# A two-layer attention and Mish network on one core: the opening of the first block rewritten, x fetched first, the queries' weights folded by raw chunks as they land

## The chip, the cores and the metric

The kernel runs on one core of one Trainium2 chip. The time is the device time of one execution in microseconds (us), as a median over several runs. The profile is of one execution of its own; its times count from the start of its span. The engines are named as the profile names them: PE is TensorE (PEld its weight loads), DVE VectorE, ACT ScalarE, POOL GpSimd, SP SyncE, which issues the DMAs.

## What is computed

Two equal layers, each an attention part and a dense part, on x of 2048 rows by 640 columns, all in float32:

```python
# attention, 32 heads of 20
q, k, v = split(layernorm(x) @ wqkv)
pq, pk  = q @ w_phi[h], k @ w_phi[h]             # per head, 20 x 20
phi     = concat(softmax(p), softmax(-p))        # 40 features a head, for pq and pk
kv, z   = phi_k.T @ v, phi_k.sum(rows)
o       = (phi_q @ kv) / (phi_q @ z + 1e-6)
x       = x + o @ wo
# dense
h = layernorm(x) @ w1 + b1                       # 1536 wide
x = x + (h * tanh(softplus(h))) @ w2
```

## The kernel before

**Tiles and parts.** The rows are worked on in 8 blocks of 256, each of two tiles of 128 rows. Every large product is done in three: each operand is split into a high part (a rounded copy by ACT) and a low part (what is left, subtracted on DVE, or on POOL for some weights), and PE adds high x high, high x low and low x high (`project_half`, L338, the matmuls at L344). One half of a projected tile is 320 columns and 5 x 3 = 15 matmuls. The rows are normed (`norm_stats` on DVE, `norm_scale` on POOL and DVE, then an ACT instruction a tile), turned on PE against the identity (`Transposed.step`, L271, transposes at L280: three steps of 4, 4 and 2), and split at L285 (`xth`, ACT) and L286 (`xtl`, DVE).

**Folding.** w_phi acts per head on q and k, so it is multiplied into their weights beforehand. `load_raw` (L212) fetches the transposed raw weights of q or k in 6 chunks: five of 120 rows (6 heads) and one of 40 rows (2 heads). `bd` holds w_phi as block-diagonal matrices, one per chunk, in six column groups of 120. `fold_phi` (L227) multiplies, for each of five k (128 rows of the weights) and for each of two halves c (three chunks each: 360 and 280 columns), a chunk by its matrix into PSUM (L237; a float32 product shows as two instructions), and then makes the high part (L242, ACT) and the low part (L243, DVE). It is run twice in layer 0: for q in the opening, and for k inside block 0. The v weights aren't folded: `load_v_weights` (L167) fetches five pieces and `split` (L123) makes the parts on ACT (L127) and DVE (L128).

**Passes.** `attend_first` (L387) goes through the blocks and makes, per tile, keys (`k`), queries (`q`) and values (`v`), in the order that `order` gives: a projection of 30 matmuls each, and for keys and queries the feature steps of `features` (L355: maxima and subtractions, an exp, sums and a scaling on DVE, POOL and ACT; the queries' first subtraction, L369, and all scalings, L379, are on POOL). The queries' features go to memory. `advance` moves the features of earlier tiles on by one step each time. Within a block, its third step norms the next block, and the later steps turn it. At the end of block 1 the folded weights are spilled and the five pieces of the output weights `wo` are fetched and split (`make_five`, L193, `make_parts`: ACT at L148, POOL at L149). `attend_second` reads the queries' features back (`average`, L569), and `dense` (L677) does the rest; neither is touched.

**Order.** The whole is planned by a scheduler that orders each engine's instructions by a simulated timeline at compile time. Where the program says `manual_schedule(engines=...)`, the named engines keep the order in which the lines stand; instructions from outside such a part can still come between. In the opening of before that holds for SP alone, so that only the DMAs are in the written order. `act` (L110) chains most of the ACT instructions one behind the other. Buffers: 5 `big`, 4 row tiles (`xn`), 2 `v`, 2 `x`; in PSUM 2 double banks `mm` and 4 single ones `one`.

The opening of before (L446 to L460), in the order of its DMAs: half of `bd`, raw chunks 0 to 2 of q, x of block 0, the rest of `bd`, chunks 3 to 5, the v weights, the raw chunks of k. The norm of block 0 comes between, then its three turning steps, the folding of q, and the parts of v, as the scheduler orders them.

Of the kernel before, what the change touches and what calls it, by code (L numbers as in the profile page):

```python
# [1 line left out]

# [6 lines left out]
F32 = mybir.dt.float32  # L9
# [32 lines left out]
def kernel(  # L42
# [25 lines left out]
    def one_tile():  # L68
        return psum.tile([P, 512], F32, tag="one", name="one", bufs=4)
# [35 lines left out]
    x1_d = dram.tile([S, D], F32, name="x1_d")  # L105
    x2_d = dram.tile([S, D], F32, name="x2_d")

    last_act = [None]

    def act(*args, **kw):  # L110

        if last_act[0] is None:
            ins = nc.scalar.activation(*args, **kw)
        else:
            with tc.issue_after(last_act[0]):
                ins = nc.scalar.activation(*args, **kw)
# [6 lines left out]
    def split(hi, lo, src, stage):  # L123

        st = stage()[:, :D]
        nc.sync.dma_start(st, src)
        nc.scalar.activation(hi, st, AF.Copy)  # L127
        nc.vector.tensor_tensor(lo, st, hi.bitcast(F32), op=ALU.subtract)  # L128

# [31 lines left out]
    def r2_pair(j):  # L161
# [2 lines left out]
            return w[:, 0], w[:, 1]  # L164
        return tuple(wts.tile([P, D], F32R, tag=f"r2{s}{j}", name=f"r2{s}{j}") for s in "hl")

    def load_v_weights():  # L167

        ws = [r1_pair(k) for k in range(KD)]
        for k in range(KD):  # L170
            split(ws[k][0][:, D:2 * D], ws[k][1][:, D:2 * D], wv[k * P:(k + 1) * P, :],
                  (row_tile, row_tile, v_tile, v_tile, big_tile)[k])
        return ws

    def load_q_weights():
# [36 lines left out]
    def load_raw(which, ts=range(6)):  # L212

        raw = []
        for t in ts:
            rows = 120 if t < 5 else 40
            if t < 5:
                r = wts.tile([P, D], F32, tag=f"r2{'hl'[which]}{5 + t}", name=f"raw{which}{t}")
            else:
                r = r2_wide(10 + which, F32)[:, 0]  # L220

            n = P if t < 5 else rows
            nc.sync.dma_start(r[:n], wqk_t[which * D + t * 120:which * D + t * 120 + n, :])
            raw.append((r, rows))
        return raw

    def fold_phi(ws, bd, raw):  # L227

        pss = {}
        for k, c in ((0, 0), (1, 0), (2, 0), (3, 0), (0, 1), (1, 1), (2, 1), (3, 1), (4, 0), (4, 1)):  # L230
            if c == 0:
                mm = None if k % 2 else mm_tile()
                pss[k] = [one_tile(), one_tile()] if k % 2 else [mm[:, 0], mm[:, 1]]
            ps = pss[k][c]
            for t in range(3 * c, 3 * c + 3):
                r, rows = raw[t]
                nc.tensor.matmul(ps[:, (t % 3) * 120:(t % 3) * 120 + rows],  # L237
                                 r[:rows, k * P:(k + 1) * P], bd[:rows, t, :rows],
                                 start=True, stop=True)
            n0, n1 = (0, 360) if c == 0 else (360, D)  # L240
            hi, lo = ws[k][0][:, n0:n1], ws[k][1][:, n0:n1]
            nc.scalar.activation(hi, ps[:, :n1 - n0], AF.Copy)  # L242
            nc.vector.tensor_tensor(lo, ps[:, :n1 - n0], hi.bitcast(F32), op=ALU.subtract)  # L243


    def norm_stats(t, xt):
# [135 lines left out]
    def fetch(x_src, b, xt=None):  # L382
        xt = x_tile() if xt is None else xt
        nc.sync.dma_start(xt, row_block(x_src, b))
        return xt

    def attend_first(layer, x_src, first):  # L387


        def fetch_normed(b):  # L390
            if layer:
                return load_turned(n2_d[b], [row_tile] * 3)
            xt = fetch(x_src, b)
            norm_scale(b, [norm_stats(t, xt) for t in range(BT)])
            return xt

# [9 lines left out]
        def keys(xts, i, v):  # L406
            e = big_tile()
            yield from features(project(xts, i % BT, kv_ws, 0), e, False)
            yield
            if i % BT == 0 and BT < i < NT - BT:  # L410
                yield
            for r in range(9):
                for j in range(4):
                    h = 3 * (4 * (r // 3) + j) + r % 3
                    if h < H:
                        nc.tensor.matmul(kva[32 * j:32 * j + DH + 1, 40 * r:40 * r + 40],  # L416
                                         v[:, (DH + 1) * h:(DH + 1) * (h + 1)], e[:, 40 * h:40 * h + 40],
                                         start=(i == 0 and r == 0), stop=(i == NT - 1), skip_group_check=True)
# [25 lines left out]
            yield  # L444

        if first is None:  # L446
            with tc.manual_schedule(engines={mybir.EngineType.SP}):
                bd = big_tile()[:120, :720].rearrange("p (t c) -> p t c", t=6)
                nc.sync.dma_start(bd[:, :3], phi_bd[:, :3])
                raw = load_raw(0, range(3))  # L450
                xt = fetch_normed(0)
                nc.sync.dma_start(bd[:, 3:], phi_bd[:, 3:])
                raw += load_raw(0, range(3, 6))
                nxt = normed(0, xt).all()
                q_ws = [r2_pair(k) for k in range(KD)]
                fold_phi(q_ws, bd, raw)
                kv_ws = load_v_weights()
                raw = load_raw(1)
            nc.sync.dma_start(mask, bass.AP(tensor=head_mask.tensor, offset=head_mask.offset,
                                            ap=[[1, 120], [120 * (DH + 1), 3]]))  # L460
        else:
            nxt, kv_ws = first
            load_k_weights(kv_ws)
            q_ws = load_q_weights()
        for b in range(NB):
            xts = nxt
            order = ("k0", "k1", "v0", "v1", "q0", "q1")
            if b == 0 and layer:
                order = ("v0", "k0", "k1", "v1", "q0", "q1")
            elif b == 0:  # L470
                order = ("v0", "q0", "v1", "k0", "q1", "k1")
            elif b == 1 and not layer:
                order = ("k0", "q0", "k1", "v0", "q1", "v1")
            elif b == NB - 1:
                order = ("k0", "k1", "v0", "v1", "q0")
            vs = [v_tile() for _ in range(BT)]
            for n, (kind, t) in enumerate(order):
                t = int(t)
                i = b * BT + t
                if b == 0 and n == (1 if layer else 3):  # L480
                    if layer == 0:
                        fold_phi(kv_ws, bd, raw)
                    kva = one_tile()
                    nc.vector.memset(kva[:, :360], 0.0)
                if b == NB - 1 and n == 3:
                    loaded = {0: load(0)}
                if b + 1 < NB:
                    if n == 0:
                        xt = fetch_normed(b + 1)
                    elif n == 2:  # L490
                        nxt = xt if layer else normed(b + 1, xt)
                    elif n > 2:
                        nxt.step()
                g = {"k": lambda: keys(xts, i, vs[t]), "q": lambda: queries(xts, i),
                     "v": lambda: values(xts, i, vs[t])}[kind]()
# [399 lines left out]
```

## Time and profile before

| | us |
|---|---|
| median of 3 runs (1381.08 to 1383.7) | 1382.19 |
| the profiled execution's own time | 1381.04 |
| its span | 1379.0 |
| busy in it: PE, DVE, ACT, POOL | 1364.3, 1077.0, 583.3, 441.0 |
| first instruction of PE starts at | 4.42 |
| PE's first long projection work (L344) starts at | 18.61 |

A busy time is the sum of an engine's instructions; those of PE are pipelined, with modelled ends, so a busy PE isn't PE at its peak, and instructions of one kind are better compared from start to start. Rows of instructions in order of time give start, duration, engine, line, operation, output and input names, shapes, count, and in brackets the idle time before them with what ended it. Rows by stretches give, per engine, busy time and count, and then the granted PE clock, the DMA engines' share and GB/s. A DMA row has the time that SP takes to issue it; "to landing" counts from that issue to the arrival.

### The profile page before, as it was taken

What the parts mean: (1) busy time and instruction counts of PE and PEld (TensorE: products, weight loads), DVE (VectorE), ACT (ScalarE), POOL (GpSimd) and SP (SyncE); (2) the same over time, 40 slices, a digit from 0 to 9 for tenths busy, and PEclk for the clock granted to TensorE, in tenths of its full rate; (3) what the DMA queues carried; (4) which work ended last, traced back from release to release, by engine and by line L of the source; (5) the groups of instructions that cost most, each with busy time, mean ns of one, the idle gap of its engine ahead of it and who ended that gap; (6) DMA issues with size and microseconds to landing.
All of it is one profiled execution on the core that took longest, in us unless ns stands there. A gap on an engine that the chain in (4) does not pass through costs nothing.

```text
span 1379.0 us, 30804 instructions
## 1 busy us (share of the span) xinstructions
PE 1364.3 (99%) x12866; PEld 1350.7 (98%) x12866; DVE 1077.0 (78%) x1820; ACT 583.3 (42%) x971; POOL 441.0 (32%) x334
## 2 busy tenths in 40 slices
PE   7999999999999999999999999999999999999998
PEld 7999999999999999999999999999999999999998
DVE  5799977886698887788769898988668776677775
ACT  4444434222355444545454333432235444354443
POOL 1353543353322221222234434453342111111112
PEclk9999999999999999999999999999999999999999
DMA  8532433779624533344473433458965321333200
GB/s 321 173 67 62 73 54 61 211 227 316 227 68 96 115 90 62 80 116 96 117 262 74 95 59 59 70 117 274 297 239 163 77 53 45 97 96 96 77 20 19
DMA packets 350277, 169.67 MB, mean 123 GB/s; under 512 B 287098, under 2 KB 323690, under 8 KB 350138
## 3 DMA queue, kind: packets, MB, share of 16 engines
q1 hardware_dynamic: 350137, 167.72, 45.0%
q8 instruction: 100, 1.64, 0.5%
q14 instruction: 40, 0.32, 0.1%
HBM read 104.76 MB, written 62.91 MB: 122 GB/s over the span
## 4 chain that ended last, share of the span: by engine, by line
PE 94%; DVE 2%; DMA 1%; issue 1%; POOL 0%; SPq 0%; ACT 0%; DVEq 0%; POOLq 0%; ACTq 0%
PE mm L344 26%; PE one L691 24%; PE mm L733 24%; PE one L344 12%; PE mm L569 3%; PE one L280 2%; PE one L416 2%; PE mm L237 1%; DMA raw<-in_wqk_t 1%; DVE m L368 1%; PE one L237 0%; DMA v<-in_wv 0%; DVE big L371 0%; DVE r L377 0%; DMA raw<-in_wo 0%
## 5 line engine op out<-in xcount | busy, mean ns | idle before, releaser
L733 PE MATMUL mm<-r2h,ol 128*128 128x320 f32 x1280 | 305.0, 309 | 0.3 <-ACT ol L716 0.3
L717 POOL TENSOR_TENSOR ol<-big,ol 128x512 fp32r<-128x512 f32 (+1 forms) x98 | 130.4, 1330 | 483.6 <-ACT ol L716 407.4
L691 PE MATMUL one<-xtl,r1h 128*128 128x256 f32 x960 | 268.2, 279 | 0.0
L691 PE MATMUL one<-xth,r1l 128*128 128x256 f32 x960 | 268.0, 279 | 0.0
L691 PE MATMUL one<-xth,r1h 128*128 128x256 f32 x960 | 265.9, 279 | 0.0
L733 PEld LDWEIGHTS mm<-r2h,ol 128*128 128x128 f32 x1280 | 219.2, 188 | 0.6 <-ACT ol L716 0.6
L733 PE MATMUL mm<-r2l,ol 128*128 128x320 f32 x640 | 197.3, 309 | 0.0
L344 PE MATMUL mm<-r1h,xth 128*128 128x320 f32 x600 | 187.5, 312 | 0.0
L344 PE MATMUL mm<-r1h,xtl 128*128 128x320 f32 x600 | 185.8, 310 | 0.4 <-DVE xtl L286 0.4
L344 PE MATMUL mm<-r1l,xth 128*128 128x320 f32 x600 | 186.0, 310 | 0.0
L691 PEld LDWEIGHTS one<-xtl,r1h 128*128 128x128 f32 x960 | 180.4, 188 | 0.0
L691 PEld LDWEIGHTS one<-xth,r1l 128*128 128x128 f32 x960 | 180.4, 188 | 0.0
L691 PEld LDWEIGHTS one<-xth,r1h 128*128 128x128 f32 x960 | 179.6, 188 | 0.0
L706 DVE TENSOR_SCALAR big<-big 128x512 f32<-128x512 f32 (+1 forms) x98 | 56.4, 575 | 110.6 <-ACT big L704 110.4
L379 POOL TENSOR_TENSOR r<-r,r 128x1280 f32<-128x1280 f32 x32 | 76.6, 2395 | 154.3 <-DVE r L378 148.5
L733 PEld LDWEIGHTS mm<-r2l,ol 128*128 128x128 f32 x640 | 120.2, 188 | 0.0
L708 ACT ACTIVATE big<-big,two 128x512 f32<-128x512 f32 (+1 forms) x98 | 70.3, 717 | 116.0 <-DVE big L707 116.0
L704 ACT ACTIVATE big<-one,b1s 128x256 f32<-128x256 f32 x192 | 81.0, 468 | 90.1 <-PE one L691 89.6
L716 ACT ACTIVATE ol<-big 128x512 fp32r<-128x512 f32 (+1 forms) x98 | 61.0, 623 | 136.3 <-DVE big L715 136.2
L344 PEld LDWEIGHTS mm<-r1h,xth 128*128 128x128 f32 x600 | 112.7, 188 | 0.8
L344 PEld LDWEIGHTS mm<-r1h,xtl 128*128 128x128 f32 x600 | 112.7, 188 | 0.7 <-DVE xtl L286 0.6
L344 PEld LDWEIGHTS mm<-r1l,xth 128*128 128x128 f32 x600 | 112.8, 188 | 0.1
(128 smaller groups left out, 3124.0 us busy)
## 6 DMA issues: line engine op xcount, KB each, us to landing
e_d<-r SPq DMA_DIRECT2D x128, 160.0 KB, 4.0
big<-e_d SPq DMA_DIRECT2D x32, 640.0 KB, 7.3
x_d<-xt SPq DMA_DIRECT2D x23, 640.0 KB, 3.6
xt<-x_d SPq DMA_DIRECT2D x22, 640.0 KB, 4.4
n_d<-xn SPq DMA_DIRECT2D x176, 80.0 KB, 2.3
xt<-in_x SPq DMA_DIRECT2D x16, 640.0 KB, 6.8
xn<-x_d SPq DMA_DIRECT2D x28, 320.0 KB, 4.4
v<-n_d SPq DMA_DIRECT2D x30, 256.0 KB, 3.1
```

Source lines behind the costliest of these rows:

```text
L280: nc.tensor.transpose(ps[:, c, t * P:(t + 1) * P], self.rows[t][:, (c0 + c) * P:(c0 + c + 1) * P], ident)
L344: nc.tensor.matmul(ps[:, :HC], a[:, sl], r, start=(k == 0 and n == 0), stop=(k == KD - 1 and n == 2))
L379: nc.gpsimd.tensor_tensor(eg, eg, r.unsqueeze(2).to_broadcast([P, 2 * H, DH]), op=ALU.mult)
L416: nc.tensor.matmul(kva[32 * j:32 * j + DH + 1, 40 * r:40 * r + 40], v[:, (DH + 1) * h:(DH + 1) * (h + 1)], e[:, 40 * h:40 * h + 40], start ...
L569: nc.tensor.matmul(po[64 * q:64 * q + 64, c, GW * j:GW * j + w], phs[g][:n, s0:s0 + 64], kvb[:n, g, :w], start=True, stop=True)
L691: nc.tensor.matmul(ph[:, j, :], l, r, start=(n == 0), stop=(n == 3 * KD - 1))
L704: exps[0] = nc.scalar.activation(part(ta, 0)[:, j - js.start], ph[:, j, :], AF.Exp, bias=b1s[:, 2 * pr + j:2 * pr + j + 1]).ins
L706: nc.vector.tensor_scalar_min(e, e, E_CAP)
L708: nc.scalar.activation(r, n, AF.Ln, bias=two)
L716: nc.scalar.activation(ah[:, js], n, AF.Copy)
L717: nc.gpsimd.tensor_tensor(al[:, js], n, ah[:, js].bitcast(F32), op=ALU.subtract)
L733: nc.tensor.matmul(pys[t][:, c, :HC], l[:, j, sl], r, start=(f == 0 and n == 0), stop=(f == KF - 1 and n == 2))
```

## The change

The opening becomes one part with a written order on all five engines (`written`, in which `act` chains nothing either):

- 30 transposes of the identity against itself go to PE first, into a bank that nobody reads.
- The DMAs: x of block 0, half of `bd`, raw chunks 0 to 2 of q, the rest of `bd`, chunks 3 to 5, the five v pieces, the raw chunks of k, x of block 1.
- The chunks have 6, 6, 6, 6, 4 and 4 heads: 120 rows, and 80 for the last two. The last matrix of `bd`, 80 x 80 now, is cleared on DVE and filled by two small DMAs. The number of folding matmuls is the same.
- The first half (chunks 0 to 2) is folded chunk by chunk for k = 0 to 3. Then follow the parts of k = 0, the two row tiles of the norm (the second on DVE, before on ACT), the parts of k = 1 and 2, a turning step, the parts of k = 3, a second step, the folding of k = 4, the third step, its parts, and the first half of q0's projection.
- The second half is folded for each k, its parts are made, and behind each but the first stand the parts of one v piece; then the second half of q0's projection and the last v piece.

Block 0 then takes q0 first (`q0, v0, v1, k0, q1, k1`; before `v0, q0, v1, k0, q1, k1`), with its projection done. The keys' folding uses the new chunks as well. Besides, in layer 0 the parts of the output weights aren't made at the end of block 1 but one piece in each of the blocks 2 to 6, behind the last chained ACT instruction; the first three fetches stay there.

The diff, cut to its core:

```diff
+    warm = one_tile()
+    for _ in range(30):
+        nc.tensor.transpose(warm[:, :P], ident, ident)
...
+    @contextmanager
+    def written():
+        in_written[0] = True
+        with tc.manual_schedule(engines={getattr(mybir.EngineType, e) for e in (
+                "PE", "SP", "Activation", "DVE", "Pool")}):
+            yield
+        in_written[0] = False
...
-        if last_act[0] is None:
+        if last_act[0] is None or in_written[0]:
             ins = nc.scalar.activation(*args, **kw)
...
-    def load_o_weights():
-        return list(make_five(KD, lambda k: wo[k * P:(k + 1) * P, :]))[1:]
...
-            rows = 120 if t < 5 else 40
+            rows = 120 if t < 4 else 80
...
-            nc.sync.dma_start(r[:n], wqk_t[which * D + t * 120:which * D + t * 120 + n, :])
+            c0 = which * D + (t * 120 if t < 5 else D - rows)
+            nc.sync.dma_start(r[:n], wqk_t[c0:c0 + n, :])
...
+    def fold_part(ps, k, t, bd, raw):
+        r, rows = raw[t]
+        n = 120 * (t % 3) if t < 5 else 200
+        nc.tensor.matmul(ps[:, n:n + rows], r[:rows, k * P:(k + 1) * P], bd[:rows, t, :rows],
+                         start=True, stop=True)
+
+    def fold_end(ws, ps, k, c):
+        n0, n1 = (0, 360) if c == 0 else (360, D)
+        hi, lo = ws[k][0][:, n0:n1], ws[k][1][:, n0:n1]
+        nc.scalar.activation(hi, ps[:, :n1 - n0], AF.Copy)
+        nc.vector.tensor_tensor(lo, ps[:, :n1 - n0], hi.bitcast(F32), op=ALU.subtract)
...
-            xt = fetch(x_src, b)
+            xt = fetch(x_src, b) if b > 1 else early
...
-            with tc.manual_schedule(engines={mybir.EngineType.SP}):
+            with written():
+                xt = fetch(x_src, 0)
                 bd = big_tile()[:120, :720].rearrange("p (t c) -> p t c", t=6)
                 nc.sync.dma_start(bd[:, :3], phi_bd[:, :3])
-                raw = load_raw(0, range(3))
-                xt = fetch_normed(0)
-                nc.sync.dma_start(bd[:, 3:], phi_bd[:, 3:])
-                raw += load_raw(0, range(3, 6))
-                nxt = normed(0, xt).all()
+                raw_q = load_raw(0, range(3))
+                nc.vector.memset(bd[:80, 5, :80], 0.0)
+                nc.sync.dma_start(bd[:40, 5, :40], phi_bd[80:120, 4, 80:120])
+                nc.sync.dma_start(bd[40:80, 5, 40:80], phi_bd[:40, 5, :40])
+                nc.sync.dma_start(bd[:, 3:5], phi_bd[:, 3:5])
+                raw_q += load_raw(0, range(3, 6))
+                kv_ws = [r1_pair(k) for k in range(KD)]
+                raw_v = [fetch_v(k) for k in range(KD)]
+                raw = load_raw(1)
+                early = fetch(x_src, 1)
+                mvs = [norm_stats(t, xt) for t in range(BT)]
+                norm_scale(0, mvs)
                 q_ws = [r2_pair(k) for k in range(KD)]
-                fold_phi(q_ws, bd, raw)
-                kv_ws = load_v_weights()
-                raw = load_raw(1)
+                mm = [mm_tile(), mm_tile()]
+                pcs = [mm[0][:, 0], mm[0][:, 1], mm[1][:, 0], mm[1][:, 1], one_tile()]
+                for t in range(3):
+                    for k in range(KD - 1):
+                        fold_part(pcs[k], k, t, bd, raw_q)
+                fold_end(q_ws, pcs[0], 0, 0)
+                xn = [row_tile() for _ in range(BT)]
+                act(xn[0], xt[:, 0, :], AF.Identity, bias=stats[:, 0, 1, 0:1], scale=stats[:, 0, 0, 0:1])
+                nc.vector.tensor_scalar(xn[1], xt[:, 1, :], stats[:, 0, 0, 1:2], stats[:, 0, 1, 1:2],
+                                        op0=ALU.mult, op1=ALU.add)
+                fold_end(q_ws, pcs[1], 1, 0)
+                fold_end(q_ws, pcs[2], 2, 0)
+                nxt = Transposed(xn)
+                nxt.step()
+                fold_end(q_ws, pcs[3], 3, 0)
+                nxt.step()
+                for t in range(3):
+                    fold_part(pcs[4], 4, t, bd, raw_q)
+                nxt.step()
+                fold_end(q_ws, pcs[4], 4, 0)
+                mm = mm_tile()
+                q0 = [mm[:, 0], mm[:, 1], mm]
+                project_half(q0[0], nxt, 0, q_ws, 0, 0)
+
+                def make_v(k):
+                    split(kv_ws[k][0][:, D:2 * D], kv_ws[k][1][:, D:2 * D], raw_v[k])
+
+                for k in range(KD):
+                    ps = one_tile()
+                    for t in range(3, 6):
+                        fold_part(ps, k, t, bd, raw_q)
+                    fold_end(q_ws, ps, k, 1)
+                    if k > 0:
+                        make_v(k - 1)
+                project_half(q0[1], nxt, 0, q_ws, 0, 1)
+                make_v(KD - 1)
...
-                order = ("v0", "q0", "v1", "k0", "q1", "k1")
+                order = ("q0", "v0", "v1", "k0", "q1", "k1")
...
+            if 2 <= b < 2 + KD and not layer:
+                with tc.issue_after(last_act[0]):
+                    o_ws.append(next(o_gen))
...
-                o_ws = load_o_weights()
+                o_gen = make_five(KD, lambda k: wo[k * P:(k + 1) * P, :])
+                next(o_gen)
+                o_ws = list(o_gen) if layer else []
```

More of the change, by code (lines that the diff above doesn't have):

```diff
@@ L1 @@
-from contextlib import ExitStack
+from contextlib import ExitStack, contextmanager
 import concourse.bass as bass
@@ L121, in v_tile, with split @@
         return work.tile([P, VW], F32, tag="v", name="v", bufs=2)
-    def split(hi, lo, src, stage):
-        st = stage()[:, :D]
-        nc.sync.dma_start(st, src)
+    def split(hi, lo, st):
         nc.scalar.activation(hi, st, AF.Copy)
@@ L165, in r2_pair, with fetch_v @@
         return tuple(wts.tile([P, D], F32R, tag=f"r2{s}{j}", name=f"r2{s}{j}") for s in "hl")
+    def fetch_v(k):
+        st = (row_tile, row_tile, v_tile, v_tile, big_tile)[k]()[:, :D]
+        nc.sync.dma_start(st, wv[k * P:(k + 1) * P, :])
+        return st
     def load_v_weights():
@@ L170, in load_v_weights @@
         for k in range(KD):
-            split(ws[k][0][:, D:2 * D], ws[k][1][:, D:2 * D], wv[k * P:(k + 1) * P, :],
-                  (row_tile, row_tile, v_tile, v_tile, big_tile)[k])
+            split(ws[k][0][:, D:2 * D], ws[k][1][:, D:2 * D], fetch_v(k))
         return ws
@@ L235, in fold_phi @@
             for t in range(3 * c, 3 * c + 3):
[L236 to L243, printed above, removed]
+                fold_part(ps, k, t, bd, raw)
+            fold_end(ws, ps, k, c)
     def norm_stats(t, xt):
@@ L493, in attend_first @@
                         nxt.step()
-                g = {"k": lambda: keys(xts, i, vs[t]), "q": lambda: queries(xts, i),
+                g = {"k": lambda: keys(xts, i, vs[t]), "q": lambda: queries(xts, i, q0 if i == 0 and not layer else None),
                      "v": lambda: values(xts, i, vs[t])}[kind]()
```

2 lines of the change are left out of this document (1 added, 1 removed).

## Prediction

> **What bounds the kernel now.** I read the page first: how much of the span TensorE (PE) is busy.
>
> ```profile
> span 1379.0 us, 30804 instructions
> PE 1364.3 (99%) x12866; PEld 1350.7 (98%) x12866; DVE 1077.0 (78%) x1820; ACT 583.3 (42%) x971; POOL 441.0 (32%) x334
> ```
>
> PE idles 1379.0 - 1364.3 = 14.7 us. Second view, the waits of PE over the whole span (total, times, longest):
>
> ```profile
> PE mm L237 <- DMA raw<-in_wqk_t: 7.9, 3, 4.4
> PE mm L569 <- PE mm L569: 0.9, 2, 0.4
> PE mm L344 <- DVE xtl L286: 0.4, 1, 0.4
> ```
>
> Of the idle time 7.9 us are waits of the first folding (L237) for its raw weight chunks. After that PE is starved by VectorE (DVE) once, for 0.4 us. So the change can give no more than the opening holds, plus whatever PE work disappears. Third view, PE in order of time in the opening:
>
> ```profile
> 4.42 1.18 PE L237 MATMUL mm<-big,raw 120*128 120x120 f32 x4 [4.42 <-DMA raw<-in_wqk_t]
> 6.41 2.08 PE L237 MATMUL mm<-big,raw 120*128 120x120 f32 x8 [0.81 <-DMA raw<-in_wqk_t]
> 11.19 2.21 PE L237 MATMUL mm<-big,raw 120*128 120x120 f32 x8 [2.70 <-DMA raw<-in_wqk_t]
> 16.29 1.70 PE L280 MATMUL one<-ident,xn 128*128 128x128 f32 x7
> 17.78 1.06 PE L237 MATMUL mm<-big,raw 120*128 120x120 f32 x6
> ```
>
> Two things are to be seen. PE has done only 4 + 8 = 12 of its 60 first folding instructions by 11.19 us. And the pace changes: 8 instructions take 2.08 and 2.21 us (0.26 each and more), the 7 transposes 17.78 - 16.29 = 1.49 (0.21 each), the next six are through in 1.06; a like six goes in 0.66 later (35.70 to 36.36, below). The granted clock says 1.00 all along (the third number from the end in the next rows), so the slow pace shows in the instructions alone.
>
> Fourth view, the instructions of L344 (projections), L237 (folding) and L280 (transposes), each counted up to 26.80 us:
>
> ```profile
> 0.00:26.80 26.80, 5.18 (x30) 1.00 0.94 332
> 0.00:26.80 26.80, 12.70 (x60) 1.00 0.94 332
> 0.00:26.80 26.80, 2.60 (x10) 1.00 0.94 332
> ```
>
> At 26.80 us PE has behind it 60 folding instructions, 10 transposes and 30 projection matmuls. That is just the PE content of the block that the change writes out by hand (both halves of the queries' folding for five k, three transposing steps, two halves of q0), without the constant's turns. So the question of the opening is: **at which time T has the changed kernel done that same set?** Its gain there is 26.8 - T.
>
> **The opening, worked out.** The constant's 30 transposes start behind the identity (about 1.4 us, an estimate) and need no data. At 0.21 to 0.26 us each they fill PE until 7.7 to 9.2 us, and less if the pace rises on the way, as it did before by 17.78 us. I take 7.3 us, when the first chunk comes. The landings follow (issues, and us from issue to landing of the three first chunks, then of x):
>
> ```profile
> 1.23 1.31 SPq L223 DMA_DIRECT2D raw<-in_wqk_t  x3
> DMA to landing us min/median/max: 3.1/4.7/5.1
> 2.58 0.43 SPq L384 DMA_DIRECT2D xt<-in_x  x1
> DMA to landing us min/median/max: 6.9/6.9/6.9
> ```
>
> Before, chunk 0 landed at 1.23 + 3.1 = 4.3, chunk 2 at 2.54 - 0.43 + 5.1 = 7.2, x at 2.58 + 6.9 = 9.5 us. The change sends the same transfers (half of the folding matrix, three chunks, x) with x at the head, so the last of them, now chunk 2, lands where x did: **9.5 us** (bounds 7.2, and 10.5 by as much again as a transfer). x took 2.3 us more than chunk 2, so ahead of chunk 0 it moves that from 4.3 to 6.6 or a little more: 7.3. x itself lands between 4.3 and 6.6: I take 5.3. The memset, two tiny transfers and the rest of the matrix come behind these on SP, ahead of chunks 3 to 5, for some 0.45 us of issue each, while transfers already queued keep the DMA engines at work: nothing. At the 332 GB/s of the rows above, 0.13 + 0.86 MB of matrix and chunks 3 to 5 need 3.0 us more (12.5 us), and the five v chunks 1.0 each (17.5 us).
>
> The statistics of x, at the durations of before:
>
> ```profile
> 9.54 1.67 DVE L250 BATCH_NORM_STATS2 bn<-xt 128x6 f32<-128x320 f32 x4
> ...
> 12.70 0.23 DVE L262 SCALAR_TENSOR_TENSOR stats<-mv,stats 128x1 f32<-128x1 f32 x2 [1.24 <-POOL stats L260]
> ```
>
> From 9.54 to 12.93, 3.4 us: done at 8.7, hidden under chunk 2. From 9.5 us on the written order binds ACT and DVE, instruction by instruction. Their pitch, start to start, is read from dense stretches:
>
> ```profile
> 13.72 0.91 ACT L116 ACTIVATE xn<-xt,stats 128x640 f32<-128x640 f32 x1
> 19.66 0.74 ACT L127 ACTIVATE r1h<-big 128x640 fp32r<-128x640 f32 x1
> 20.29 0.48 ACT L242 ACTIVATE r2h<-mm 128x360 fp32r<-128x360 f32 x1
> 20.35 1.02 DVE L286 TENSOR_TENSOR xtl<-one,xth 128x512 fp32r<-128x512 f32 x2
> 22.02 0.82 DVE L128 TENSOR_TENSOR r1l<-big,r1h 128x640 fp32r<-128x640 f32 x1
> 22.75 0.53 DVE L243 TENSOR_TENSOR r2l<-mm,r2h 128x360 fp32r<-128x360 f32 x1
> 23.19 1.24 DVE L243 TENSOR_TENSOR r2l<-one,r2h 128x360 fp32r<-128x360 f32 x3
> ```
>
> DVE: 640 columns 0.73 (22.02 to 22.75), 360 columns 0.44 (22.75 to 23.19), 280 columns 0.36 (between the half of the first and the second), a 512 and a 256 together 1.0. ACT: 640 columns 0.63 (19.66 to 20.29), others as their rows.
>
> - k0's first fold ends and ACT starts at 9.95; its copy and row tile 0 take it to 11.3. DVE, behind its part of k0, writes row tile 1 by 11.5 (no row has it: between 0.36 and 0.73, and 0.6 taken, nearest to the like width).
> - The first transposes end by 12.1, ACT has xth at 12.7, DVE then xtl at 13.45, and in the written order fold 3 at 13.9, the second xtl at 14.5, the third at 14.8, fold 4 at 15.3.
> - q0's first half waits at k = 4 for that last one: done at 15.8. Behind it on PE's queue stand the second folds, though their chunks landed at 12.5; who waits for them are ACT and DVE. The first fold ends at 16.5, and DVE, idle from 15.3, resumes at 17.2.
> - Now DVE takes five second parts with three of the v weights' parts between: 5 x 0.36 + 3 x 0.73 = 4.0, and 0.6 of hand-overs, to 21.8. The v chunks (17.5) aren't late for it.
> - q0's second half ends 0.5 later: **T = 22.3**, and the gain is 26.8 - 22.3 = **4.5 us**.
>
> Bounds: no T before chunk 5 and what needs it, 30 folds at 0.11 and 30 projections at 0.146 (row of the chain below), 7.7 together; from 11.2, where the last chunk of before came, 18.9, a gain of 7.9. On the other side, if each of some 15 hand-overs between engines costs 0.2 more, T is 25.3 and the gain 1.5.
>
> What raises the pace is the open price here. The trace has the pace rise right behind seven transposes, but at the end of 6.6 us without a break (11.19 to 17.78), folds among them. [...]
>
> **Chunks of 6, 4, 4 heads.** The number of instructions stays. The 40-row piece goes:
>
> ```profile
> 31.75 4.10 PE one L344 x28
> 35.70 0.82 PE L237 MATMUL mm<-big,raw 120*128 120x120 f32 x6
> 36.36 0.83 PE L237 MATMUL one<-big,raw 120*128 120x120 f32 x6
> 39.25 0.70 PE L237 MATMUL one<-big,raw 120*128 120x120 f32 x4
> 39.89 0.41 PE L237 MATMUL one<-big,r 40*128 40x40 f32 x2
> 40.23 0.70 PE L237 MATMUL mm<-big,raw 120*128 120x120 f32 x4
> 302.94 1.38 PE L569 MATMUL mm<-kvb,big 120*64 120x63 f32 x40
> 304.15 0.27 PE L569 MATMUL mm<-kvb,ol 80*64 80x42 f32 x4
> 304.25 1.36 PE L569 MATMUL mm<-kvb,big 120*64 120x63 f32 x40
> ```
>
> Six pieces of 120 rows take 0.66 us start to start; four of 120 and two of 40 take 40.23 - 39.25 = 0.98, though they multiply less. In the second attention pass 80 rows behind 120 open no such gap: four in 304.25 - 304.15 = 0.10. So I expect 0.66 for a new second half, 0.32 less. For the queries that is in T already; for the keys' folding, in PE's unbroken path, it is 5 x 0.32 = **1.6 us**, between 0 (the gap stays) and 1.6.
>
> **Elsewhere.** The 0.4 us wait is DVE's, which is full there (columns: PE, PEld, DVE, ACT, POOL):
>
> ```profile
> 80.00:100.00 20.00, 19.58 (x308) 18.73 (x307) 20.00 (x28) 8.30 (x12) 12.77 (x8) 1.00 0.32 52
> 140.00:160.00 20.00, 20.00 (x256) 19.74 (x255) 16.66 (x27) 6.04 (x9) 11.03 (x8) 1.00 0.23 37
> L149 POOL TENSOR_TENSOR r2l<-raw,r2h x4: 1576/1578/1582, 44.1 to 61.0; 128x640 fp32r<-128x640 f32 x4
> 32.53 1.55 DVE L368 TENSOR_REDUCE m<-r 128x32 f32<-128x640 f32 x2 [3.78 <-ACT r L116]
> ```
>
> q0's maxima start at 32.53 there; with q0 ready at T they start some 9 us earlier, so DVE has them behind it before it fills up. The output weights' parts, 1.58 us each on POOL (four of the five at 44 to 63 us), leave that stretch too. I count 0.3 of the 0.4. They go to blocks 2 to 6, one a block, where POOL has 9 us free in 20 and PE has no wait: nothing. Sum: 4.5 + 1.6 + 0.3 = 6.4. The profiled execution took 1381.0 us (span 1379.0 and 2.0 around it) and becomes 1374.6; the median of the three runs is 1382.2, 1.2 above it, so on its scale the forecast is 1382.2 - 6.4 = **1375.8**.
>
> **The rivals.**
> - *The constant doesn't raise the pace.* For it: the seven transposes ran slow themselves. Against: the rise came right behind them. The folds then go at 0.26 from 7.3 us; k0's last is the 18th, 7.3 + 18 x 0.26 = 12.0 in place of 10.0, and all behind it comes 2.0 later: 1377.8.
> - *More gain.* Instructions from outside the written part may be put between its own; v0's matmuls then fill PE's gaps, and T counts near its bound: 26.8 - 19.5 + 1.9 = 9.2, so 1373.0. Against: q0's halves themselves wait for DVE.
> - *DVE keeps its time.* If its steps aren't drawn forward with q0, PE waits for xtl near 90 us until DVE is there, and the gain is eaten up to 0 to 2 us: 1381.2. For it: 20.00 of 20 busy. Against: the 3.78 us that it idled ahead of 32.53.
> - *Slower: the output weights in blocks 2 to 6.* Each puts 1.58 us ahead of a feature's step on POOL and some 0.7 on ACT. If POOL ends last there, five blocks lose 5 x 2.3 = 11.5, less the 6.4: 1387.3. It turns slower once PE waits for xtl by over 6.4 / 5 = 1.3 us a block. Against: PE is full there and POOL half idle.
>
> **Chances.** Forecast 0.57 (own range 1374 to 1378); no rise of pace 0.13; more gain 0.13; DVE 0.09; slower 0.08. A measurement of this kernel tells some 0.2% (2.8 us) from no change, so 1379.4 is the border. Faster: 0.57 + 0.13 + 0.13, less 0.06 for the late tails of the first two, 0.77; same 0.09 + 0.06 = 0.15; slower 0.08. The range of 1371.5 to 1380.5 leaves out most of DVE's case, the slower one and the far ends.
>
> **What would show it.** The 60, 10 and 30 instructions counted by 22.3 us; folds at some 0.11 us from 7.3 us on; second halves of the keys' folding at 0.66; no wait of PE for xtl at 70 to 100 us, none in 110 to 260. It is wrong if chunk 2 lands after 11 us, if folds go at 0.26 until 12 us, or if PE idles behind T for the v weights.

## The result

The changed kernel took 1377.92 us (median of 7 runs, 1376.53 to 1379.83); the kernel before, run beside it, 1381.16 (7 runs). The ratio is 0.9969 [0.996, 0.9979], or 4.3 us of 1381; the two medians lie 3.2 us apart, and in the profiled executions the span went from 1379.0 to 1375.0, by 4.0. Forecast were 6.4. The forecast of 1375.8 is 2.1 us too low, and the range holds the time. Part of that nearness is luck: the median of before, 1382.19 when the forecast was built on it, came out 1.0 lower in the seven runs beside the changed kernel, and the medians' gain is only half of the forecast. The page after:

```profile
span 1375.0 us, 30860 instructions
PE 1362.1 (99%) x12896; PEld 1349.8 (98%) x12896; DVE 1073.3 (78%) x1822; ACT 581.3 (42%) x970; POOL 441.0 (32%) x334
```

PE idles 12.9 us now instead of 14.7, though 5.1 us of its busy time are the turns of the identity, which yield nothing. What it waits for (total, times, longest) is another list than before:

```profile
PE mm L364 <- DVE r1l L251: 1.6, 1, 1.6
PE one L89 <- POOL ident masks.py:199: 1.3, 1, 1.3
PE one L364 <- ACT r1h L137: 0.9, 1, 0.9
PE one L300 <- ACT xn L126: 0.9, 1, 0.9
PE mm L244 <- DVE r1l L251: 0.9, 1, 0.9
PE mm L244 <- DMA raw<-in_wqk_t: 0.9, 1, 0.9
PE mm L637 <- PE mm L637: 0.9, 2, 0.4
PE one L300 <- ACT xth L129: 0.7, 1, 0.7
```

The 7.9 us behind raw chunks are down to 0.9, and the wait for `xtl` is gone. New are two waits for `r1l` of the folding (L251), the low parts of the keys' folded weights: 0.9 and 1.55 us. Nothing in the forecast had them.

**Where the time went, mark by mark.** Three marks carry the account. The first is the keys' folding. In before it begins at 35.70 us; the rows count the projection matmuls (L344) and the foldings (L237) begun by then, the one that starts at the edge among them:

```profile
0.00:35.70 35.70, 14.08 (x90) 1.00 0.87 313
0.00:35.70 35.70, 12.71 (x61) 1.00 0.87 313
```

The same lines after (now L364 and L244), at 31.06 us:

```profile
0.00:31.06 31.06, 14.01 (x90) 1.00 0.97 331
0.00:31.06 31.06, 8.29 (x67) 1.00 0.97 331
```

PE has the same 90 projection matmuls behind it, and 66 foldings against 60: six of the keys' are already done, which cost 0.67 us in a row. So the opening gave 35.70 + 0.67 - 31.06 = **5.3 us**. The second and third marks are the first average of the second pass and the first matmul of the dense part of layer 1; each row gives the start of its first instruction behind the three durations. Before:

```profile
L569 PE MATMUL mm<-kvb,big x640: 222/222/270, 264.4 to 343.7; 120*64 120x63 f32 x160
L691 PE MATMUL one<-xth,r1h x960: 274/280/283, 368.5 to 1363.4; 128*128 128x256 f32 x192
```

After:

```profile
L637 PE MATMUL mm<-kvb,big x640: 222/222/269, 259.6 to 338.9; 120*64 120x63 f32 x160
L759 PE MATMUL one<-xth,r1h x960: 274/280/283, 363.6 to 1359.4; 128*128 128x256 f32 x192
```

The lead is 4.8 us at the first average, 4.9 at the dense part, 4.0 when the last such matmul starts. Up to the first average the sum closes: 5.3 of the opening, 1.6 of the keys' second halves (below), 0.4 of `xtl`, less 0.9 + 1.55 of the new waits, is 4.85. Another 0.9 is lost in layer 2, which the change hardly touches: the last such matmul of layer 1 still starts 4.9 earlier (690.0 against 694.9).

**The opening against its steps.** PE in order of time, after:

```profile
1.34 5.11 PE L89 MATMUL one<-ident 128*128 128x128 f32 x30 [1.34 <-POOL ident masks.py:199]
6.60 1.12 PE L244 MATMUL mm<-big,raw 120*128 120x120 f32 x8
8.62 2.04 PE L244 MATMUL mm<-big,raw 120*128 120x120 f32 x16 [0.90 <-DMA raw<-in_wqk_t]
...
16.67 0.61 PE L244 MATMUL one<-big,raw 120*128 120x120 f32 x4
...
18.68 0.64 PE L244 MATMUL mm<-big,raw 120*128 120x120 f32 x4
...
20.42 0.38 PE L244 MATMUL mm<-big,raw 120*128 120x120 f32 x2
...
33.06 0.58 PE L244 MATMUL mm<-big,raw 120*128 120x120 f32 x4
...
33.70 0.61 PE L244 MATMUL one<-big,raw 120*128 120x120 f32 x4
...
36.10 0.67 PE L244 MATMUL mm<-big,raw 120*128 120x120 f32 x4 [0.90 <-DVE r1l L251]
...
40.31 0.42 PE L364 MATMUL mm<-r1h,xth 128*128 128x320 f32 x1 [1.55 <-DVE r1l L251]
```

The turns end at 6.45, the foldings follow at 0.13 us each, all 24 are done by 10.7, and the second of the second-half foldings starts, the first being through, at 16.67 (16.5 in the forecast). The six instructions at 18.68 and 20.42 are the first of the keys' folding, put between the queries'. By the forecast's own count the opening came out as told: up to 22.3 us PE has begun 10 turning transposes, 31 projection matmuls and 66 foldings, where 10, 30 and 60 were forecast. But six of the 31 are v0's, put into gaps, and the last of q0's own starts at 25.19. A new second half takes 33.70 - 33.06 = 0.64, against 0.98 before. The turns themselves, in stretches of 1 us (the fourth number from the end, in brackets, is how many matmuls run in the stretch, those that reach in from before among them), show the pace rise; from start to start it is 0.21 us up to 4.59 and 0.11 from 4.76 on:

```profile
2.30:3.30 1.00, 1.00 (x6) 1.00 0.79 292
4.30:5.30 1.00, 1.00 (x9) 1.00 1.02 269
5.30:6.30 1.00, 1.00 (x11) 1.00 0.90 292
```

The granted clock stays at 1.00 in all of them, so this rise shows in the starts and the count alone.

**The new waits.** VectorE after, in order of time:

```profile
17.30 0.45 DVE L251 TENSOR_TENSOR r2l<-one,r2h 128x280 fp32r<-128x280 f32 x1 [1.72 <-ACT r2h L250]
...
21.52 0.45 DVE L251 TENSOR_TENSOR r2l<-one,r2h 128x280 fp32r<-128x280 f32 x1
...
27.50 1.53 DVE L388 TENSOR_REDUCE m<-r 128x32 f32<-128x640 f32 x2
...
33.68 1.49 DVE L397 TENSOR_REDUCE r<-r 128x64 f32<-128x1280 f32 x1 [1.50 <-ACT r L129]
35.09 0.52 DVE L251 TENSOR_TENSOR r1l<-one,r1h 128x360 fp32r<-128x360 f32 x1
...
38.30 1.61 DVE L270 BATCH_NORM_STATS2 bn<-xt 128x6 f32<-128x320 f32 x4
39.82 0.43 DVE L251 TENSOR_TENSOR r1l<-mm,r1h 128x280 fp32r<-128x280 f32 x1
```

And ScalarE after:

```profile
32.39 1.26 ACT L129 ACTIVATE r<-r 128x1280 f32<-128x1280 f32 x1
33.55 0.46 ACT L250 ACTIVATE r1h<-one 128x360 fp32r<-128x360 f32 x1
```

The exp of q0 (L129, 128x1280) stands on ACT ahead of the copies of the keys' weights (L250), though the folding that the copy at 33.55 takes was through by 31.72; and the sums of q0 (L397), which wait 1.50 us for that exp, stand on DVE ahead of the low parts (L251). Only one copy and its low part, those of the six early foldings, come before them (at 21.83 and 26.03). The second wait, up to 40.31, ends with the low part of 39.82, and directly ahead of that one DVE makes the statistics of a later block (L270, 1.61 us). In before the exp and the sums came after the keys' folding. ScalarE before:

```profile
50.61 1.26 ACT L116 ACTIVATE r<-r 128x1280 f32<-128x1280 f32 x1
```

VectorE before:

```profile
52.95 1.48 DVE L377 TENSOR_REDUCE r<-r 128x64 f32<-128x1280 f32 x1
```

So q0's early features seem to collide with the keys' folding. This was the theory for the experiments; the rivals were that single parts of the change are worth less than forecast.

### The profile page after: what moved, and what is told of

It is laid out like the page before. It is cut to its first block, busy times and chain, and to the rows that moved or that the text cites. A ratio compares the mean times of both kernels' runs of the same rounds, so it can differ in the third digit from the quotient of the medians.

```text
span 1375.0 us, 30860 instructions
## 1 busy us (share of the span) xinstructions
PE 1362.1 (99%) x12896; PEld 1349.8 (98%) x12896; DVE 1073.3 (78%) x1822; ACT 581.3 (42%) x970; POOL 441.0 (32%) x334
## 4 chain that ended last, share of the span: by engine, by line
PE 96%; DMA 1%; DVE 1%; ACT 0%; issue 0%; DVEq 0%; SPq 0%
PE mm L364 29%; PE one L759 24%; PE mm L801 24%; PE one L364 12%; PE mm L637 3%; PE one L300 2%; PE one L436 2%; DMA v<-in_wv 1%; DMA r1l<-wp_d 0%; DVE r1l L251 0%; DVE bn L270 0%; ACT xn L129 0%; DVE r L397 0%; DVE xt L811 0%; ACT r L129 0%
## 5 line engine op out<-in xcount | busy, mean ns | idle before, releaser
L364 PE MATMUL mm<-r1h,xth 128*128 128x320 f32 x600 | 187.6, 313 | 1.6 <-DVE r1l L251 1.6
L364 PE MATMUL mm<-r1l,xth 128*128 128x320 f32 x600 | 185.8, 310 | 0.0
L364 PE MATMUL mm<-r1h,xtl 128*128 128x320 f32 x600 | 185.6, 310 | 0.0
L364 PEld LDWEIGHTS mm<-r1h,xth 128*128 128x128 f32 x600 | 112.8, 188 | 2.6 <-DVE r1l L251 1.8
L364 PEld LDWEIGHTS mm<-r1h,xtl 128*128 128x128 f32 x600 | 112.7, 188 | 0.2
L364 PEld LDWEIGHTS mm<-r1l,xth 128*128 128x128 f32 x600 | 112.8, 188 | 0.0
```

What stands on the lines that cost most here:

```text
L364: nc.tensor.matmul(ps[:, :HC], a[:, sl], r, start=(k == 0 and n == 0), stop=(k == KD - 1 and n == 2))
```

## The experiments

All medians stand against the kernel before, run on the same chip. "Mark" is the start of the first average, read from the row shown above in each kernel's own trace (one execution).

| kernel | median us | ratio to before | mark us |
|---|---|---|---|
| before | | | 264.4 |
| after | 1377.92 | 0.9969 [0.996, 0.9979] | 259.6 |
| after_again | 1377.47 | 0.9966 [0.9953, 0.9978] | 259.2 |
| hold_exp | 1375.4 | 0.9954 [0.9941, 0.9968] | 256.8 |
| old_chunks | 1379.78 | 0.9987 [0.9976, 0.9997] | 261.0 |
| no_turns | 1379.0 | 0.9977 [0.9967, 0.9986] | 260.4 |
| o_at_once | 1380.1 | 0.9984 [0.9975, 0.9993] | 260.7 |
| order_only | 1380.91 | 0.9993 [0.9984, 1.0002] | 263.1 |
| before_chunks | 1380.39 | 0.9984 [0.9975, 0.9992] | 262.8 |
| before_turns | 1383.45 | 1.0009 [1.0, 1.0018] | 263.7 |
| hold_old_chunks | 1378.23 | 0.9972 [0.996, 0.9985] | 259.9 |
| hold_o_at_once | 1375.43 | 0.9955 [0.9942, 0.9967] | 257.3 |
| hold_no_turns | 1376.11 | 0.9956 [0.9943, 0.997] | 257.4 |
| hold_late_v | 1374.52 | 0.9948 [0.9936, 0.9961] | 257.1 |

**hold_exp.** The changed kernel, with q0's exp held back by one step of block 0's order:

```diff
-                advance()
+                if layer or b or n != 2:
+                    advance()
```

> The changed kernel, but in block 0 the features are not moved on at the third step, so that q0's exp and sums come behind the folding of the keys. Theory: in the changed kernel PE's new waits of 0.9 and 1.6 us at 35 to 40 us come from q0's exp (1.26 us on ACT) and sums (1.49 us on DVE), which now stand ahead of the keys' parts; without them there the waits for r1l fall from 2.5 to 0.8 us or less and the span from 1375.0 to some 1373.2. Rival: the keys' folding at 0.66 us a half is simply too fast for the parts or the PSUM banks; then the waits stay at 2 us or more, and the span at 1375.

Of the waits of PE between 20 and 262 us, the one for `r1l`:

```profile
PE mm L244 <- DVE r1l L251: 0.2, 1, 0.2
```

The instructions of the averaging in hold_exp, whose first start is the mark:

```profile
L638 PE MATMUL mm<-kvb,big x640: 222/222/269, 256.8 to 336.4; 120*64 120x63 f32 x160
```

The waits for `r1l` fall from 2.45 to 0.2 us and the mark comes 2.8 earlier: 2.25 of it is these waits. Another 0.56 had been gained by the keys' folding (30.50 against 31.06), where the edit does nothing: landings of that execution (the 16 foldings that wait for the raw chunks start at 7.96 there, at 8.62 in the changed kernel). The theory holds: the exp now stands at 43.25 on ACT, behind the keys' copies. The edit also changes where the scheduler puts these statistics. VectorE in hold_exp:

```profile
35.79 0.45 DVE L251 TENSOR_TENSOR r1l<-mm,r1h 128x280 fp32r<-128x280 f32 x1 [0.22 <-ACT r1h L250]
...
37.03 1.67 DVE L270 BATCH_NORM_STATS2 bn<-xt 128x6 f32<-128x320 f32 x4
```

The low part that came behind them at 39.82 now comes ahead of them. How much of the 1.55 us is due to the statistics and how much to the exp and the sums, no run separates. Of the 2.8 us the ratios show 2.1 (0.0015 of 1381) and the medians 2.5. The two intervals overlap a little, but every run of hold_exp (1375.88 at most) lies under every one of the changed kernel (1376.33 at least, after_again included).

**old_chunks, no_turns, o_at_once.** The changed kernel with one part undone each: chunks of 120 and 40 rows, no turns of the constant, the output weights at the end of block 1. With the old chunks the rest of `bd` comes in one transfer again, too.

```diff
-            rows = 120 if t < 4 else 80
+            rows = 120 if t < 5 else 40
-        n = 120 * (t % 3) if t < 5 else 200
+        n = 120 * (t % 3)
```
```diff
-    warm = one_tile()
-    for _ in range(30):
-        nc.tensor.transpose(warm[:, :P], ident, ident)
```
```diff
-            if 2 <= b < 2 + KD and not layer:
-                with tc.issue_after(last_act[0]):
-                    o_ws.append(next(o_gen))
...
-                o_ws = list(o_gen) if layer else []
+                o_ws = list(o_gen)
```

> The changed kernel with the old chunks, five of 120 rows and one of 40. Theory: the second halves of the keys' folding take 0.98 us again, 1.6 us more of PE's path, but ACT and DVE set the end of the keys' parts there, so the waits for r1l shrink by the same 1.6 and the span stays within 0.7 us of 1375.0: in the changed kernel as it stands the new chunks are worth nothing. Rival: their 1.6 us count in full, and the span is 1376.6 or more.

> The changed kernel without the 30 transposes of the identity. Theory: the first folds run at some 0.26 us an instruction instead of 0.13, PE's pace rises only after several us of work, the first half ends some 2 us later and the span is some 1377.0. [...]

> The changed kernel with all parts of the output weights made at the end of block 1 again. Theory: their move is worth 0.4 us at most, the wait for xtl near 90 us; span 1375.0 to 1375.5. Rival: the move is what brings the gain by clearing POOL, and the span goes back to 1378 or more.

The old chunks cost 1.4 us at the mark: the theory, which put them at nothing, is wrong. The rival's number is near, but not for its reason. The keys' folding begins at 32.38 in place of 31.06, so 1.3 us is lost before it, by the queries' halves, which neither had counted. Behind that start only 0.2 is lost, since the waits for `r1l` shrink from 2.45 to 1.3 us as PE is busy for longer ahead of them; in that the theory was nearly right. Without the turns the foldings start slow, PE in order of time:

```profile
6.41 5.45 PE L241 MATMUL mm<-big,raw 120*128 120x120 f32 x24 [6.41 <-DMA raw<-in_wqk_t]
```

24 in 5.45 us (0.23 each) against 0.13 with the turns: all are through at 11.86 instead of 10.66, 1.2 us later (the theory had 2), yet the mark moves by only 0.8, and the profiled span is 1375.0 as with the turns.

The output weights cost 1.1 at the mark, and 1.5 from the start of the keys' folding, which was 0.34 earlier in that execution (30.72). About half of it is lost where the forecast hadn't looked: one of their ACT copies stands ahead of q0's exp (at 31.78, 0.73 us), which then starts 2.00 us behind the start of the keys' folding instead of 1.33, and the first wait for `r1l` grows from 0.90 to 1.57. The second shrinks from 1.55 to 0.17, as PE comes to it later. The other half is lost in later blocks, where waits of 0.2 for `xtl` and 0.2 for `big` stand. The span, 1379.7, is the number of the rival, but 3.1 us of it are lost behind the dense part of layer 1: the lag behind the changed kernel grows from 1.2 there to 4.3 at the first average of layer 2 (932.2 against 927.9), and in between PE waits 1.9 us for `ol`. What follows the wait of 1.57 us is a surprise; the columns behind the count are the granted clock, the DMA share and GB/s:

```profile
37.00:38.00 1.00, 1.00 (x9) 0.74 1.04 394
38.00:39.00 1.00, 1.00 (x7) 0.50 1.01 384
39.00:40.00 1.00, 1.00 (x6) 0.50 1.03 397
40.00:41.00 1.00, 0.83 (x5) 0.55 1.01 389
```

The granted clock is 0.50 from about 37.5 to 40.9 us.

**order_only, before_chunks, before_turns.** Parts from the other side: the changed kernel less all three parts above (the edits of old_chunks, no_turns and o_at_once together), and the kernel before with the new chunks alone (`rows`, `n` and the transfers that go with them, as in the change), or with the turns alone (the three lines behind the identity).

> The new opening's order and q0 first alone: no turns of the identity, the old chunks, all output weights at the end of block 1. Theory, from undoing one part at a time: the second pass's first average starts at 264.4 us before and 259.6 after; the turns are worth 0.8 of it, the chunks 1.4, the output weights 1.1, so it starts at some 262.9 and the span is about 1377.5. Rival: the parts share one wait for VectorE in the keys' folding and don't add; then it starts below 261.5 or above 264.

> The kernel before with the new chunks alone. Theory: there PE works without a break from 11.2 us and nothing crowds ACT and DVE, so all ten second halves, the queries' and the keys', go from 0.98 to 0.66 us in full: 3.1 us, span 1375.9. Rival: only the keys' five count, since the queries' lie in a stretch that waits for data: 1.6 us, span 1377.4.

> The kernel before with the 30 turns of the identity alone. Theory: PE keeps the raised pace through its waits for data (0.8 and 2.7 us), so the 28 instructions from 11.2 to 17.8 us take some 3.3 us in place of 6.6: span 1375.7. Rival: the pace falls back in the 2.7 us of idle time, or data end the opening anyway: gain under 1 us, span 1378 or more.

The written order alone gives 1.3 us at the mark, almost what was expected of it, and nothing in the time that the interval could tell from none. The new chunks alone give 1.6. That is the rival's number, but again not for its reason: 0.65 is gained before the keys' folding begins (35.05 against 35.70), so the queries' halves count in part, and 0.9 behind it, less than the keys' 1.6; there the wait for `r1l` grows by 0.2, and the rest isn't accounted for. The turns alone give no time, though the mark is 0.7 earlier; the first average of layer 2 is already 1.1 later than in before (933.6 against 932.5), and why isn't known. Their theory is wrong: the 28 instructions take from 11.12 to 17.65 us, as long as before. In before_turns PE has nothing to do behind the first foldings, up to 11.12 us. The profile puts this wait down to VectorE's statistics; in before it ends at 11.19 with the raw chunks, so that data are the likelier cause. Then the granted clock falls:

```profile
9.00:10.00 1.00, 0.00 (x0) 1.00 1.09 337
...
14.00:15.00 1.00, 0.52 (x3) 0.50 1.02 389
15.00:16.00 1.00, 1.00 (x6) 0.50 1.05 399
16.00:17.00 1.00, 1.00 (x7) 0.50 1.05 399
```

**hold_old_chunks, hold_o_at_once, hold_no_turns.** The three undoings once more, on hold_exp, where no wait for the keys' parts covers them.

> q0's exp and sums held back as in hold_exp, with the old chunks. With the wait for VectorE gone, the chunks' worth should show clean: second halves of the keys' folding at 0.98 instead of 0.66, five times, so the second pass's first average starts at 256.8 + 1.6 = 258.4 us, and at up to 260.0 if the queries' halves count too. Rival: the chunks are worth nothing where ACT and DVE set the pace of the parts (0.74 and 0.73 us a pair of second half and v part): 257 or below.

> q0's exp and sums held back as in hold_exp, with all output weights at the end of block 1. Theory: the move of the output weights was worth about 1 us in the changed kernel only because an ACT copy of theirs stood in the same queue ahead of the keys' parts, in front of q0's exp; with the exp held back it costs 0.7 us at most, and the first average starts by 257.5. Rival: it holds up POOL and DVE in blocks 1 and 2 by itself: 258 or later, and waits of PE for xtl between 60 and 100 us.

> q0's exp and sums held back as in hold_exp, without the 30 turns of the identity. Theory: the turns are worth the 0.8 us that undoing them cost in the changed kernel, between its 259.6 and 260.4; so the second pass's first average starts at 256.8 + 0.8 = 257.6 us. Rival: in the changed kernel the wait for VectorE hid part of them, as it hid half of the chunks (1.4 in place of 3.1 us); then it starts at 258.5 or later.

The averaging in hold_old_chunks:

```profile
L635 PE MATMUL mm<-kvb,big x640: 222/222/269, 259.9 to 339.3; 120*64 120x63 f32 x160
```

With the old chunks the mark is 3.1 us later than in hold_exp, near the 10 x 0.32 = 3.2 of all ten second halves. But 0.4 of it is there before any of them: the first turning transposes start at 11.46 in place of 11.04. Up to the start of the keys' folding another 1.5 is lost, the queries' halves in full, and behind it 1.1, most of the keys'. So the chunks are worth 2.7 there. The 0.74 and 0.73 us of the rival are those of a v part alone: in the changed kernel a second half and a v part together take 0.91 us on ACT (18.46 to 19.37) and 1.09 on DVE (19.34 to 20.43). The output weights are worth 0.5, within what the theory allowed, of which 0.4 is the wait for `xtl` that comes back, in the waits of hold_o_at_once between 43 and 262 us:

```profile
PE mm L364 <- DVE xtl L306: 0.4, 1, 0.4
```

The turns are worth 0.6, near the 0.8 of the theory. Landings alone moved the opening by 0.56 between two executions, so the last two are sizes of that order and no finer; in the medians neither shows beyond the intervals. The chunks do show: every run of hold_old_chunks (1377.55 at least) lies over every one of hold_exp, though the intervals of the two ratios overlap.

**after_again** and **hold_late_v** ask about layer 2: the changed kernel once more, and hold_exp with the v weights' parts of the change of layers behind the last steps of the dense part, instead of behind the last exp (`tail_act` is the dense part's last copy on ACT, `tail_dve` its last step on DVE).

```diff
-                with tc.issue_after(exps[0]):
+                with tc.issue_after(tail_act[0]), tc.issue_after(tail_dve[0]):
                     kv_ws = load_v_weights()
```

> The changed kernel once more, beside the other two. Theory: the first average starts at 259.6 us, up to 0.6 earlier or later with the landing of the first chunks, with 1.5 to 2.6 us of waits of PE for r1l at 34 to 41 us; the time is 0.3% under that of before, 0.15% over that of hold_exp. Rival: what held for the first profile was chance of one execution, and the waits for r1l are under 1 us.

> The version that holds q0's exp and sums back, and besides with layer 1's v parts at the change of layers behind the last Mish steps on ACT and DVE. Theory: in several of the runs PE waits there for a Mish step that stands behind a v part whose DMA is late (0.3 to 1.9 us, and in one run the granted clock fell to half for 3 us behind it); without that the span is 1373.0 or less, and no run comes out above the others. Rival: the later v parts make layer 2's first projection wait instead: span 1374 or more.

The repeat gives nearly the same ratio, and the same waits for `r1l` (1.6 and 0.8). Its lead over before is 5.2 us at the first average but 2.5 when the last matmul of the dense part starts (1360.9): it loses 2.7 behind the mark, where the first profile of the same kernel lost 0.9. hold_late_v is the fastest kernel of all, 0.9948 [0.9936, 0.9961], but its interval overlaps that of hold_exp, its span of 1374.5 is above the 1373.0 of the theory, and layer 2 isn't settled by it. Waits of PE over its whole span:

```profile
PE one L300 <- issue: 1.8, 1, 1.8
...
PE one L364 <- ACT r1h L137: 0.6, 1, 0.6
```

The first of these lies near 932 us, in layer 2, where nothing was edited, and the wait at the change of layers is still 0.6.

## Why the prediction came out high on gain

- **What bounds the kernel: right.** The gain came from the opening's waits and the keys' folding, and the direction and the mechanism were as told.
- **The opening: mis-sized, 4.5 forecast, 5.3 measured.** Its steps held within a few tenths: the foldings at 0.13 us, not 0.11, DVE's resumption at 17.30 (17.2), the last low part done at 21.97 (21.8), and the set of instructions counted by 22.3. The difference is nearly all the six foldings of the keys (0.67), which were put into PE's gaps with matmuls of v0: the rival "more gain" came true in part. That T came out to the tenth is luck, since it was said of q0's second half, which lasted to 25.19.
- **The turns: right in what they do, and their price too high.** The rise of pace came with transposes alone: 0.21 us from start to start up to 4.59, 0.11 from 4.76 on. It doesn't always come so early: in after_again and hold_late_v the 30 take 6.4 us, 0.21 each from the first start to that of the first folding, and the foldings go at 0.12 behind them all the same. The rival had 2.0 us hang on it; undoing them costs 0.6 to 0.8, since less than the delay of the foldings reaches the end.
- **The chunks: right.** 0.64 to 0.67 for a second half, which is 1.6 for the keys' five. That the queries' 1.6 count as well stood in T without a price of its own. Both together measure 2.7 at the mark (1.5 and 1.1) where no wait for `r1l` covers them.
- **"Elsewhere": the step that failed.** It took q0's earlier features for relief alone: "with q0 ready at T they start some 9 us earlier, so DVE has them behind it before it fills up". The maxima came 5.0 earlier (27.50 against 32.53), not 9, as q0 itself was ready later than T, and the exp and the sums 18 to 19 us earlier, which brought them right ahead of the keys' copies and low parts. The wait for `xtl` did go (0.4 against 0.3). The output weights' move seems to have had more part in that than q0: with the move undone a wait of 0.2 or 0.4 comes back in o_at_once and hold_o_at_once, though none in order_only. But 2.45 us of waits for `r1l` took its place: the term is -2.05 where +0.3 stood. That this is the cause is shown by hold_exp, where one step held back removes 2.25 of the 2.45; the statistics of a later block, which it moves as well, are part of how the second wait came about. The forecast had counted how full DVE is around 80 and 140 us and never asked what stood in its queue at 33 us, when the moved work would arrive.
- **The slower rival** (output weights in blocks 2 to 6) didn't come true: no wait for `xtl` is left in the changed kernel, and the move is worth 0.5 us in hold_exp.
- **The rest, -0.9 us in layer 2, stays open.** The waits there are 0.9 for `r1h` (L137) and 0.7 for `xth` after, and 0.3 for `r1h` and 0.3 for `ol` before, which is 1.0 more. They differ between kernels and executions: 1.2 for `xth` and 1.3 for `ol` in after_again, 1.0 for `xt` in hold_exp, 1.8 near 932 us in hold_late_v. What sets them wasn't found. The forecast had no term for it, and as the same kernel lost 2.7 there in after_again, the 0.9 is the size of one execution.

With terms as measured: 5.3 + 1.6 + 0.4 - 2.45 - 0.9 = 3.95, the 4.0 us by which the spans of these two executions differ.

## What to carry to other kernels

When work is drawn forward, look at the place where it lands: which instructions of the critical chain stand behind it on each engine's queue at that moment (here the copy at 33.55 behind q0's exp on ACT, the low part at 35.09 behind its sums on DVE), not how busy the engine is on the average later. A saving that is covered by a new wait looks smaller than it is (the chunks: 1.4 us beside the collision, 2.7 without it), so remove the wait before judging the parts. A part can also be worth less alone than in company: the queries' chunks gave 0.65 us in the kernel before and 1.5 in the new order. And a rival's number that comes true isn't yet its mechanism: old_chunks and before_chunks met one at the mark, and the time lay elsewhere.

## What the runs showed of the hardware that had not been expected

- **Three idle stretches of 1.57 to 2.17 us were followed by half the granted clock.** In o_at_once 1.57 us of idle PE ahead of 36.43 were followed by a granted clock of 0.50 for some 3.4 us, though PE did work in between; 1.95 us ahead of 705.1 in the same execution were followed by it from 706.5 to 709.9; in before_turns 2.17 us ahead of 11.12 were followed by it from 14 to 17 us, with PE busy for only 0.33 and 0.52 of the two us from 13 to 15 as well. The 1.55 us ahead of 40.31 in the changed kernel were not: the clock reads 1.00 there up to 45 us.
- **The granted clock didn't show the slow opening.** In the changed kernel it reads 1.00 while the turns start every 0.21 us, as while they start every 0.11.
- **The 40-row pieces opened a gap, the 80-row ones none.** Four instructions of 120 rows and two of 40 took 0.98 us in the kernel before; four of 120 and two of 80 took 0.64 to 0.67 in the changed one, no more than six of 120 rows (0.66 before).
